# One-hots of the routing on VectorE, and another order of work where attention ends and the experts begin

## The chip, the cores and the metric

The kernel runs on one core of one Trainium2 chip. The metric is the device time of one launch in microseconds; the kernel before takes 539.12 us (median of 3 runs, 538.48 to 539.36). TensorE (PE in the profile) multiplies matrices, VectorE (DVE), ScalarE (ACT) and GpSimd (POOL) do elementwise work, SyncE (SP) issues most of the transfers. Each engine works off its own queue in order; between engines there are semaphores.

## The reference

A gated linear attention (mLSTM) over 2 batches, 8 heads, 768 steps and head size 40; then a mixture of 8 experts of which each of the 1536 tokens takes its best 2; then one wide layer for all tokens.

```python
for t in range(S):                                  # attention, per batch and head
    m_new = np.maximum(f_gate[t] + m, i_gate[t])
    C = exp(f_gate[t] + m - m_new) * C + exp(i_gate[t] - m_new) * outer(v[t], k[t])
    n = exp(f_gate[t] + m - m_new) * n + exp(i_gate[t] - m_new) * k[t]
    y[t] = sigmoid(o_gate[t]) * (C @ q[t]) / max(abs(n @ q[t]), 1.0)
logits = x @ w_gate + log1p(exp(x @ w_noise)) * noise   # x: [1536, 320]
top2, weights = two largest per token, softmax over the two
out[tokens of e] += weight * (relu(x @ w1[e]) @ w2[e])  # w1 320x1024, w2 1024x320, per expert
h = out @ w_in                                          # 320x2048
y = (h * clip(h + 3, 0, 6) / 6) @ w_out                 # 2048x320
```

## The kernel before, in words

Everything is one program with an order written out by hand: the order of the calls is the order in each engine's queue.

**Attention.** The 768 steps are cut into NT = 12 chunks of 64 steps; with two batches a chunk has 128 tokens. For chunk n the main loop (L1077) calls `pmul(n + 1)` (VectorE: scores times decay, into P), `inter(n)` (TensorE: query times the state Sb), `state(n)` (TensorE: keys times values; VectorE: the new Sb), `norm2(n - 1)` (VectorE: the finished output x of the chunk before, written to DRAM as Xd), `scores(n + 2)`, `values(n)` and `xpose(n - 1)` (TensorE: P times values; three transposes of x, L412), `expo(n + 2)` (TensorE: the exponents, its last matmuls at L271; ScalarE: dd), `logits(n - 1)` (TensorE: gate logits, L426), `kscale` (ScalarE: scaled keys kt), `norm_eg(n)` and `norm_pv(n)` (VectorE: sums and denominators; GpSimd: od). Between them `w_load`, `w_hi` and `w_lo` fetch weights of experts 0 and 1 into the four RAW buffers and split them into two parts (ScalarE and VectorE).

**Routing.** `route(m)` works on the logits of chunks 2m and 2m + 1. It is a generator: `step()` lets every running one go on to its next `yield`, and so puts a small instruction or two between the other work. It first copies the logits (zg), needs ScalarE for a softplus (u; the first VectorE operation on it is L451), finds the two largest, counts with small matmuls (L488 to L495) how many tokens each expert has so far, and gets a slot for each token and choice. Then it writes the token numbers into a table: two one-hot matrices LO (which of 128 rows) and HV (which of 32 columns, times the token number's two parts) are multiplied by four matmuls at L562, and the product is added to `slot`. `spot` counts places at which TensorE has work enough in front of the next small matmuls; a routing waits in its `yield` loop until `spot` has gone on by 2 (SPI) since its one-hots, or by SP = 4 since the last count. `until(m)` runs steps until m routings are in the table (`found`). The table of the first eight chunks (CUT) is turned into the index `idx[0]`, by which `gather` (GpSimd, an indirect transfer) fetches the x rows of the first 256 tokens of experts 0 and 1.

For routings 0 to 4 the one-hots are twelve GpSimd instructions (L541 to L544); for the last, routing 5, they are four VectorE instructions (L546 to L554).

**End of attention (L1120 to L1158).** The last two chunks are written out one call after the other: all values, norms, transposes and logits of chunks 10 and 11, `until` the table of eight chunks, `gather`, `xprep` (transposes of the gathered x, L828, and their split into XH and XL), and between them `dummy` matmuls, whose result nobody reads.

**Experts.** A unit is an expert with up to 416 tokens; expert 0 has a first unit of 256 tokens. A unit has eight steps f: `L1` (eight matmuls, L891, relu to hb by ScalarE, the remainder by VectorE, L897), and two steps later `L2` (six matmuls, L927 to L929). `bg(i, f, fn)` hangs a call behind step f of unit i, `bga` one right after its `L1`. `step` calls, weight splits (WS), gathers and the `xprep` of the next unit hang there. `open_late` gives the memory of attention to the second weight set SB.

Of the kernel before, what the change touches and what calls it, by code (L numbers as in the profile page):

```python
# [13 lines left out]
BF = mybir.dt.bfloat16  # L14
# [4 lines left out]
OP = mybir.AluOpType  # L19
# [4 lines left out]
B, H, S, D = 2, 8, 768, 40  # L24
# [19 lines left out]
LATE = 256  # L44
XP = (2, 3, 5, 6)
VSPLIT = {}
WS = ((-1, 0), (0, 3), (0, 4), (0, 5, 'h'), (1, 0, 'l'), (1, 1), (1, 1), (1, 3), (1, 5), (1, 7), (2, 1))
TROWS = CAP + 11 * 128
OVB = 22
OV = OVB * 128  # L50
# [16 lines left out]
def mlstm_moe_mlp(ctx, tc, qk, kv, on, gf, gf4, wg, nz, w1, w2, w_in, w_out, cf, cb, ci, out):  # L67
# [17 lines left out]
    def open_psd():  # L85
        nonlocal psd
        psa_cm.__exit__(None, None, None)
        psd = ctx.enter_context(tc.tile_pool(name="psd", bufs=1, space=PSUM))
# [151 lines left out]
    gens = []  # L240
    spot, counted = [0], [0, -2]

    def step(k=1):
        for _ in range(k):
            for g_ in list(gens):
                if next(g_, "end") == "end":
                    gens.remove(g_)
# [40 lines left out]
    def pmul(n):  # L288
        d = Pt[n][1]
        s4 = s4t.pop(n)  # L290
        P = att.tile([128, 8, 64], F32, name="P", bufs=3)
        V.tensor_tensor(P.rearrange("p (x a) t -> p x a t", x=2), s4, d.rearrange("p (x a) t -> p x a t", x=2), OP.mult)
        Pt[n] = P
# [41 lines left out]
    def values(n, hs):  # L335
        pv, _, vv = y_ps[n]
        for h in hs:
            for b in range(B):
                T.matmul(pv[rows[b], h, :], Pt[n][rows[b], h, :], vv[rows[b], h, :], start=True, stop=True)
# [5 lines left out]
    def dummy(k, b):  # L345
        p = bank(b)
        for _ in range(k):
            T.matmul(p, identb, cbt[:, 0:512], start=True, stop=True)
# [5 lines left out]
    def norm_eg(n):  # L354
        it = y_ps[n][1]
        y = att2.tile([128, 8, V1], F32, name="y", bufs=2)
        if n:
            V.tensor_tensor(y.rearrange("p (x a) c -> p x a c", x=2), it,
                            eG[:, n].rearrange("p (x a) -> p x a", x=2)[:, :, :, None].to_broadcast([128, 2, 4, V1]), OP.mult)
        ya[n] = y  # L360

    def norm_pv(n):
        y = ya[n]
        if n:
            V.tensor_tensor(y, y, y_ps[n][0], OP.add)
        else:
            V.tensor_copy(y, y_ps[n][0])
        o = att2.tile([128, 8, D], F32, name="od", bufs=2)
        G.tensor_tensor(o, ont[:, n].rearrange("p (h d) -> p h d", h=8), y[:, :, 0:D], OP.mult)
        step()  # L370
        den = att.tile([128, 8], F32, name="den", bufs=2)
        V.tensor_scalar(den, y[:, :, D], -1.0, 1.0, OP.mult, OP.max)
        step()
        V.tensor_tensor(den, den, y[:, :, D], OP.max)
        step()
        rd = att.tile([128, 8], F32, name="rd", bufs=2)
        V.reciprocal(rd, den)
        step()
        yt[n] = o, rd

    def norm2(n):
        o, rd = yt[n]
        x = att2.tile([128, XW], F32, name="x", bufs=4)
        V.tensor_tensor(x[:, 0:DM].rearrange("p (a x d) -> p x a d", a=4, x=2), o.rearrange("p (x a) d -> p x a d", x=2),
                        rd.rearrange("p (x a) -> p x a", x=2)[:, :, :, None].to_broadcast([128, 2, 4, D]), OP.mult)
        A.copy(x[:, DM:XW], x[:, 256:DM])
        xt[n] = x
        nc.sync.dma_start(Xd[n * 128:(n + 1) * 128], x)
# [9 lines left out]
    SLE = const.tile([128, NT, 2], I32, name="SLE")  # L398
    SLY = const.tile([128, NT, 2], I32, name="SLY")
    WAB = const.tile([128, NT, 2], F32, name="WAB")  # L400
    run = const.tile([128, E], BF, name="run")
    V.memset(run, 0.0)
    adj = const.tile([128, E], F32, name="adj")
# [4 lines left out]
    def xpose(n, b=6):  # L408
        p = bank(b)
        for k in range(3):  # L410
            w = 128 if k < 2 else 64
            T.transpose(p[0:w, k * 128:k * 128 + 128], xt[n][:, k * 128:k * 128 + w], ident)  # L412
        t = att2.tile([128, 3, 128], F32, name="xT", bufs=2)
        A.copy(t[:, 0:2], p[:, 0:256].rearrange("p (k t) -> p k t", k=2))
        A.copy(t[0:64, 2], p[0:64, 256:384])
        xT[n] = t
# [19 lines left out]
    def small(shape, name, dt=F32, bufs=2):  # L436
        return const.tile(shape, dt, name=name, bufs=bufs)

    def route(m):
# [95 lines left out]
        V.scalar_tensor_tensor(lh[:, 1], sli, 7, h1, OP.bitwise_and, OP.bitwise_or)  # L535
        LO = small([128, 4, 128], "LO", BF, 1)
        HV = small([128, 4, 2, 32], "HV", BF, 1)
        if m < NT // 2 - 1:
            lf = small([128, 2, 4], "lf")
            V.tensor_copy(lf, lh)  # L540
            for j in range(4):  # L541
                G.tensor_scalar(LO[:, j], iota128, lf[:, 0, j:j + 1], None, OP.is_equal)
                for x, v in enumerate((pcol, nval[:, 2 * m + j // 2:2 * m + j // 2 + 1])):
                    G.tensor_scalar(HV[:, j, x], iota128[:, 0:32], lf[:, 1, j:j + 1], v, OP.is_equal, OP.mult)  # L544
        else:
            V.tensor_tensor(LO, iota128[:, None, :].to_broadcast([128, 4, 128]),  # L546
                            lh[:, 0, :, None].to_broadcast([128, 4, 128]), OP.is_equal)
            yield
            H = small([128, 4, 32], "H", BF, 1)
            V.tensor_tensor(H, iota128[:, None, 0:32].to_broadcast([128, 4, 32]),  # L550
                            lh[:, 1, :, None].to_broadcast([128, 4, 32]), OP.is_equal)
            yield
            V.tensor_scalar(HV[:, :, 0], H, pcol, None, OP.mult)
            V.tensor_tensor(HV[:, :, 1].rearrange("p (n k) c -> p n k c", n=2), H.rearrange("p (n k) c -> p n k c", n=2),  # L554
                            nval[:, 2 * m:2 * m + 2, None, None].to_broadcast([128, 2, 2, 32]), OP.mult)
        at = spot[0]
        yield
        while spot[0] < at + SPI and not now[0]:
# [296 lines left out]
    def xprep(u, i, b=5):  # L855
        if u.e < 8:
            xsplit(u, i, XG[:, (u.xo + i) % 4], u.tiles[i][1], b)
        else:
            xsplit(u, i, x2t[4 * (u.e - 8) + i], 128, b)
# [215 lines left out]
    expo(1)  # L1075
    scores(1)
    for n in range(NT - 2):  # L1077
        pmul(n + 1)
        step(2)
        inter(n)  # L1080
        state(n)
        if n == 1:
            later_exponents()
            G.tensor_copy(adj, iota8)
        if n + 4 < NT:
            load_qk(n + 4)
        if 0 < n < NT - 3:
            load_kv(n + 3)
        if n % 2 == 0 and n + 2 < NT:
            load_on(n + 2)  # L1090
        if n >= 1:
            norm2(n - 1)
            step()
        w_lo(WL[n] if n < len(WL) else 0)
        scores(n + 2)
        values(n, range(8))
        if n >= 1:
            xpose(n - 1)
        expo(n + 2)
        for _ in range(WD[n] if n < len(WD) else 0):  # L1100
            w_load()
        w_hi(WH[n] if n < len(WH) else 0)
        if n == 1:
            decays(4, NT)
        if n + 3 >= NT:
            dummy(DUM[0], 4)
        if n >= 1:
            logits(n - 1)
        kscale(n + 2)
        if n == 0:  # L1110
            for i in range(3):
                gate(0, i)
        for i in ((0,), (1, 2))[n % 2]:
            gate(n // 2 * 2 + 2, i)
        norm_eg(n)
        step(2)
        norm_pv(n)
        if n >= 2 and n % 2 == 0:
            gens.append(route(n // 2 - 1))
# [6 lines left out]
    w_load()  # L1126
    step()
    values(n, range(8))
    norm_eg(n)
    step(2)  # L1130
    inter(n + 1, 4, s4p)
    norm_pv(n)
    spot[0] += 2
    norm_eg(n + 1)
    step(2)
    values(n + 1, range(8))
    open_psd()
    xpose(n - 1)
    norm2(n)
    norm_pv(n + 1)  # L1140
    spot[0] += 2
    xpose(n, 5)
    logits(n - 1)
    until(CUT[0] // 2)
    gather(units[0])
    norm2(n + 1)
    gens.append(route(NT // 2 - 2))
    dummy(DUM[1], 2)
    logits(n)
    dummy(DUM[2], 2)  # L1150
    xpose(n + 1, 6)
    step(3)
    xprep(units[0], 0, 3)
    logits(n + 1)
    gens.append(route(NT // 2 - 1))
    dummy(DUM[3], 5)
    xprep(units[0], 1, 2)
    dummy(DUM[4], 6)  # L1158

    LAG = 2  # L1160

    def bg(i, f, fn, *a):
        units[i].bg.setdefault(f, []).append((fn, a))
# [27 lines left out]
        sets[1] = Halves(late, "SB")  # L1191
        xbufs(late, 1)

    open_late()
    bg(0, 0, gather, units[1])
    for f in range(8):
        bg(0, f, step, 6)
    for i, f, *c in WS:
        for g_ in {'h': (w_hi,), 'l': (w_lo, w_load)}[c[0]] if c else (w_split,):
            if i < 0:  # L1200
                g_()
            else:
                bg(i, f, g_)
    bg(0, 7, until, NT // 2)
    bg(1, 1, gather, units[2])
    bg(1, 2, gather, units[3], 0, 1)
    bg(1, 7, gather, units[3], 2, 3)
    for i in range(3, M0 - 1):
        bg(i, 0, gather, units[i + 1])
# [139 lines left out]
```

## Time and profile before

| | us |
|---|---|
| median of 3 runs (lowest, highest) | 539.12 (538.48, 539.36) |
| the profiled execution | 538.7 |
| its span, first to last instruction | 536.9 |
| first matmul of expert 0 (L891) | 123.44 |
| TensorE busy | 494.1 |
| VectorE busy | 341.1 |
| ScalarE busy | 231.7 |
| GpSimd busy | 129.2 |

Busy time is the time in which an engine has at least one instruction in work; matmuls overlap, so a busy TensorE is not one at its peak. "Idle before" an instruction is the time that its engine had nothing to do ahead of it, with the instruction that released it. The granted clock is given as a share of 2.4 GHz: 0.50 is 1.2 GHz. Times in the rows below are us from the start of the span unless they are marked ns.

### The profile page before, as it was taken

What the parts mean: (1) busy time and instruction counts of PE and PEld (TensorE: products, weight loads), DVE (VectorE), ACT (ScalarE), POOL (GpSimd) and SP (SyncE); (2) the same over time, 40 slices, a digit from 0 to 9 for tenths busy, and PEclk for the clock granted to TensorE, in tenths of its full rate; (3) what the DMA queues carried; (4) which work ended last, traced back from release to release, by engine and by line L of the source; (5) the groups of instructions that cost most, each with busy time, mean ns of one, the idle gap of its engine ahead of it and who ended that gap; (6) DMA issues with size and microseconds to landing.
All of it is one profiled execution on the core that took longest, in us unless ns stands there. A gap on an engine that the chain in (4) does not pass through costs nothing. (4 is left out here: it accounts for less than half of the span.)

```text
span 536.9 us, 11617 instructions
## 1 busy us (share of the span) xinstructions
PE 494.1 (92%) x4547; PEld 449.1 (84%) x4547; DVE 341.1 (64%) x874; ACT 231.7 (43%) x483; POOL 129.2 (24%) x178
## 2 busy tenths in 40 slices
PE   5799867868699999999999999989999999999996
PEld 2687656646699999999999999979989899899985
DVE  7547766727476587878787877468697434353433
ACT  2346547215254454545454553255564334333322
POOL 2434455263330420202111002377400100000000
PEclk9555555559699999999999999999999999999999
DMA  9858663233277479888988769697722600010011
GB/s 187 206 170 234 167 191 117 71 95 93 79 219 219 151 271 292 290 284 290 273 302 275 267 183 319 205 295 227 241 99 80 214 0 1 1 31 20 13 37 49
DMA packets 41531, 90.76 MB, mean 169 GB/s; under 512 B 5233, under 2 KB 23985, under 8 KB 41473
## 3 DMA queue, kind: packets, MB, share of 16 engines
q1 hardware_dynamic: 34960, 69.07, 41.1%
q0 software_dynamic: 5696, 19.67, 11.9%
q10 hardware_dynamic: 816, 1.25, 1.1%
q8 instruction: 36, 0.59, 0.5%
q14 instruction: 23, 0.18, 0.1%
HBM read 67.16 MB, written 22.68 MB: 167 GB/s over the span
## 5 line engine op out<-in xcount | busy, mean ns | idle before, releaser
L906 DVE SCALAR_TENSOR_TENSOR r<-r,bank 128x512 f32<-128x512 f32 (+1 forms) x56 | 34.2, 611 | 80.1 <-ACT r L905 79.6
L894 ACT ACTIVATE hb<-bank 128x416 fp32r<-128x416 f32 (+2 forms) x80 | 35.6, 446 | 95.9 <-PE bank L891 82.7
L905 ACT ACTIVATE r<-bank,cft 128x512 f32<-128x512 f32 (+1 forms) x56 | 35.0, 626 | 95.5 <-PE bank L891 92.3
L891 PE MATMUL bank<-XH,SB 128*128 128x416 f32 (+3 forms) x280 | 75.6, 340 | 0.3 <-PEq L991 0.3
L891 PE MATMUL bank<-XL,SB 128*128 128x416 f32 (+3 forms) x192 | 66.9, 349 | 0.0
L818 POOL DMA_INDIRECT XG<-Xd,idx x32 | 33.1, 1034 | 127.5 <-PE bank L828 116.7
L927 PE MATMUL bank<-SB,hb 128*128 128x320 f32 x192 | 61.9, 322 | 1.0 <-ACT hb L878 1.0
L927 PE MATMUL bank<-SA,hb 128*128 128x320 f32 x192 | 61.3, 319 | 0.0
L929 PE MATMUL bank<-SA,hb 128*128 128x320 f32 x192 | 59.7, 311 | 0.1
L928 PE MATMUL bank<-SA,hb 128*128 128x320 f32 x192 | 59.6, 310 | 0.0
L929 PE MATMUL bank<-SB,hb 128*128 128x320 f32 x192 | 59.3, 309 | 0.0
L928 PE MATMUL bank<-SB,hb 128*128 128x320 f32 x192 | 59.2, 308 | 0.0
L891 PEld LDWEIGHTS bank<-XH,SB 128*128 128x128 f32 x280 | 50.3, 189 | 4.6 <-issue 0.6
L891 PE MATMUL bank<-XH,SA 128*128 128x416 f32 (+2 forms) x200 | 51.2, 329 | 0.1
L891 PE MATMUL bank<-XL,SA 128*128 128x416 f32 (+2 forms) x120 | 39.3, 329 | 0.1
L891 PEld LDWEIGHTS bank<-XH,SA 128*128 128x128 f32 x200 | 36.5, 196 | 1.9 <-ACT XH L829 0.6
L927 PEld LDWEIGHTS bank<-SB,hb 128*128 128x128 f32 x192 | 36.2, 188 | 2.1 <-ACT hb L878 1.2
L891 PEld LDWEIGHTS bank<-XL,SB 128*128 128x128 f32 x192 | 36.2, 188 | 2.0
L927 PEld LDWEIGHTS bank<-SA,hb 128*128 128x128 f32 x192 | 36.4, 190 | 1.1
L928 PEld LDWEIGHTS bank<-SA,hb 128*128 128x128 f32 x192 | 36.4, 190 | 0.9
L928 PEld LDWEIGHTS bank<-SB,hb 128*128 128x128 f32 x192 | 36.2, 189 | 0.6
L929 PEld LDWEIGHTS bank<-SA,hb 128*128 128x128 f32 x192 | 36.3, 189 | 0.3 <-DVE hb L879 0.3
(225 smaller groups left out, 1113.8 us busy)
## 6 DMA issues: line engine op xcount, KB each, us to landing
raw<-in_w_dram SPq DMA_DIRECT2D x18, 640.0 KB, 4.8
raw<-in_w_dram SPq DMA_DIRECT2D x18, 512.0 KB, 5.6
craw<-in_w_in_dram SPq DMA_DIRECT2D x8, 640.0 KB, 6.4
craw<-in_w_out_dram SPq DMA_DIRECT2D x8, 640.0 KB, 6.4
raw<-in_w_dram SPq DMA_DIRECT2D x18, 256.0 KB, 4.3
qk<-in_qk_dram SPq DMA_DIRECT2D x22, 192.0 KB, 4.3
Yd<-yo SPq DMA_DIRECT2D x24, 160.0 KB, 4.6
kv<-in_kv_dram SPq DMA_DIRECT2D x11, 324.0 KB, 5.0
```

The costliest lines, as they stand in the source:

```text
L818: G.indirect_dma_start(out=XG[0:n, (u.xo + i) % 4, :], out_offset=None, in_=Xd[0:CUT[u.i] * 128] if early else Xd[:, :], in_offset=bass.In ...
L891: T.matmul(p, a, b, start=(i == 0), stop=(i == 7))
L894: A.activation(hb[:, 0:N], p, AF.Relu)
L905: A.activation(r, p, AF.Relu, bias=three)
L906: V.scalar_tensor_tensor(r, r, 6.0, p, OP.min, OP.mult)
L927: T.matmul(p, h, wh, start=s, stop=False)
L928: T.matmul(p, h, wl, start=False, stop=False)
L929: T.matmul(p, hb[:, lo:lo + n], wh, start=False, stop=t)
```

## The change

1. The one-hots of all routings are made by VectorE. The slot halves go to bf16 (`lf`), a bf16 copy of the row numbers 0 to 127 (`iotab`, copied once by GpSimd in chunk 1) replaces the fp32 one, and there are four more `yield`s between the instructions.
2. In chunk 9 `step` counts double (`pace`) until chunk 11's values, `spot` goes on by two more, and the two dummies are gone.
3. The end of attention has another order: transposes of chunk 9 right after the values of chunk 10, then `until` and the `gather` for expert 0, its `xprep` ahead of the values of chunk 11, and expert 0 behind the transposes of chunk 10. All dummies are gone.
4. The logits of chunk 10, output, transposes and logits of chunk 11 and the last routing hang in expert 0's first three steps, and so does `open_late`. The weight splits, the `until` for all routings and the gathers for the later units hang one step or two later.

```diff
-WS = ((-1, 0), (0, 3), (0, 4), (0, 5, 'h'), (1, 0, 'l'), (1, 1), ...)
+WS = ((0, 2), (0, 3), (0, 4), (0, 6, 'h'), (1, 0, 'l'), (1, 1), ...)
+    pace = [1]
     def step(k=1):
-        for _ in range(k):
+        for _ in range(k * pace[0]):
...
-        if m < NT // 2 - 1:
-            lf = small([128, 2, 4], "lf")
-            V.tensor_copy(lf, lh)
-            for j in range(4):
-                G.tensor_scalar(LO[:, j], iota128, lf[:, 0, j:j + 1], None, OP.is_equal)
-                for x, v in enumerate((pcol, nval[:, 2 * m + j // 2:2 * m + j // 2 + 1])):
-                    G.tensor_scalar(HV[:, j, x], iota128[:, 0:32], lf[:, 1, j:j + 1], v, OP.is_equal, OP.mult)
-        else:
-            V.tensor_tensor(LO, iota128[:, None, :].to_broadcast([128, 4, 128]),
-                            lh[:, 0, :, None].to_broadcast([128, 4, 128]), OP.is_equal)
...
+        yield
+        lf = small([128, 2, 4], "lf", BF)
+        V.tensor_copy(lf, lh)
+        yield
+        V.tensor_tensor(LO, iotab[:, None, :].to_broadcast([128, 4, 128]),
+                        lf[:, 0, :, None].to_broadcast([128, 4, 128]), OP.is_equal)
+        yield
+        H = small([128, 4, 32], "H", BF, 1)
+        V.tensor_tensor(H, iotab[:, None, 0:32].to_broadcast([128, 4, 32]),
+                        lf[:, 1, :, None].to_broadcast([128, 4, 32]), OP.is_equal)
+        yield
+        V.tensor_scalar(HV[:, :, 0], H, pcol, None, OP.mult)
+        V.tensor_tensor(HV[:, :, 1]..., H..., nval[:, 2 * m:2 * m + 2, ...], OP.mult)
...
     for n in range(NT - 2):
+        if n == NT - 3:
+            pace[0] = 2
...
+            G.tensor_copy(iotab, iota128)
...
-        if n + 3 >= NT:
-            dummy(DUM[0], 4)
...
+        if n == NT - 3:
+            spot[0] += 2
         step(2)
...
     values(n, range(8))
+    xpose(n - 1)
     norm_eg(n)
-    step(2)
     inter(n + 1, 4, s4p)
-    norm_pv(n)
-    spot[0] += 2
-    norm_eg(n + 1)
-    step(2)
-    values(n + 1, range(8))
-    open_psd()
-    xpose(n - 1)
-    norm2(n)
-    norm_pv(n + 1)
-    spot[0] += 2
-    xpose(n, 5)
-    logits(n - 1)
     until(CUT[0] // 2)
     gather(units[0])
-    norm2(n + 1)
+    norm_pv(n)
+    logits(n - 1)
     gens.append(route(NT // 2 - 2))
-    dummy(DUM[1], 2)
-    logits(n)
-    dummy(DUM[2], 2)
-    xpose(n + 1, 6)
-    step(3)
-    xprep(units[0], 0, 3)
-    logits(n + 1)
-    gens.append(route(NT // 2 - 1))
-    dummy(DUM[3], 5)
-    xprep(units[0], 1, 2)
-    dummy(DUM[4], 6)
+    norm_eg(n + 1)
+    spot[0] += 2
+    step(2)
+    norm2(n)
+    xprep(units[0], 0, 6)
+    xprep(units[0], 1, 5)
+    values(n + 1, range(8))
+    pace[0] = 1
+    open_psd()
+    xpose(n)
+    norm_pv(n + 1)
...
-    open_late()
+    bga(0, 0, logits, n)
+    bga(0, 0, norm2, n + 1)
+    bga(0, 1, xpose, n + 1, 5)
+    bga(0, 2, logits, n + 1)
+    bga(0, 2, last_route)
     bg(0, 0, gather, units[1])
+    bg(0, 2, open_late)
     for f in range(8):
         bg(0, f, step, 6)
+    bg(1, 0, step, 8)
...
-    bg(0, 7, until, NT // 2)
-    bg(1, 1, gather, units[2])
-    bg(1, 2, gather, units[3], 0, 1)
+    bg(1, 1, until, NT // 2)
+    bg(1, 2, gather, units[2])
+    bg(1, 3, gather, units[3], 0, 1)
```

## Rows read from the trace of the kernel before

**Rows 1.** The page: busy time of the engines, and the granted TensorE clock in 40 slices.

```profile
PE 494.1 (92%) x4547; PEld 449.1 (84%) x4547; DVE 341.1 (64%) x874; ACT 231.7 (43%) x483; POOL 129.2 (24%) x178
...
PEclk9555555559699999999999999999999999999999
```

**Rows 2.** Waits of TensorE, whole span: total us, times, longest.

```profile
PE bank L562 <- POOL HV L544: 24.8, 19, 2.7
```

**Rows 3.** Windows of two stretches: busy time and instructions of each engine, clock, DMA.

```profile
57.00:69.00 12.00, 12.00 (x268) 9.82 (x270) 11.31 (x43) 6.50 (x20) 3.64 (x4) 0.50 0.63 181
69.00:76.00 7.00, 2.82 (x84) 2.28 (x88) 1.72 (x11) 4.12 (x14) 5.95 (x12) 0.50 0.73 197
```

**Rows 4.** Timeline of TensorE, chunks 3 to 7: start, duration, instructions, [idle before, releaser].

```profile
36.27 0.61 PE L271 MATMUL bank<-RWG,SEL 128*128 128x64 bf16 x8
...
41.56 0.87 PE L412 MATMUL bank<-cft,x 128*128 128x128 f32 x3
...
59.60 0.90 PE L412 MATMUL bank<-cft,x 128*128 128x128 f32 x3
...
68.03 0.61 PE L271 MATMUL bank<-RWG,SEL 128*128 128x64 bf16 x8
...
72.64 0.21 PE L562 MATMUL bank<-HV,LO 128*128 128x64 bf16 x1 [1.27 <-POOL HV L544]
...
78.48 0.90 PE L412 MATMUL bank<-cft,x 128*128 128x128 f32 x3
```

**Rows 5.** Timeline of VectorE, chunks 3 and 7.

```profile
39.92 0.18 DVE L451 TENSOR_SCALAR w<-u 128x16 f32<-128x16 f32 x1 [1.53 <-ACT u L446]
...
40.92 0.48 DVE L384 TENSOR_TENSOR x<-od,rd 128x320 f32<-128x320 f32 x1
...
72.97 0.22 DVE L451 TENSOR_SCALAR w<-u 128x16 f32<-128x16 f32 x1 [2.79 <-ACT u L446]
```

**Rows 6.** Groups of GpSimd by line: busy us, mean ns, idle before.

```profile
L544 POOL TENSOR_SCALAR HV<-cft,lf 128x32 bf16<-128x32 f32 x40 | 18.4, 469 | 0.0
L542 POOL TENSOR_SCALAR LO<-cft,lf 128x128 bf16<-128x128 f32 x20 | 12.8, 640 | 8.9 <-DVE lf L540 7.3 <-DVE rd L377 1.1 <-DVE den L374 0.4
```

**Rows 7.** Timeline of VectorE: the one-hots of the last routing.

```profile
141.94 0.69 DVE L546 TENSOR_TENSOR LO<-cft,lh 128x512 bf16<-128x512 f32 x1
...
142.87 0.29 DVE L550 TENSOR_TENSOR H<-cft,lh 128x128 bf16<-128x128 f32 x1
...
143.60 0.24 DVE L553 TENSOR_SCALAR HV<-H,cft 128x128 bf16<-128x128 bf16 x1
143.76 0.28 DVE L554 TENSOR_TENSOR HV<-H,cft 128x128 bf16<-128x128 bf16 x1
```

**Rows 8.** Groups of TensorE by line, end of the attention part.

```profile
L348 PE MATMUL bank<-cbt 128*128 128x512 bf16 x10 | 4.5, 548 | 0.7 <-ACT dd L274 0.7
```

**Rows 9.** Timeline of TensorE, end of the attention part.

```profile
118.68 0.66 PE L426 MATMUL bank<-wgt,xT 128*32 128x16 f32 x24
...
120.10 0.85 PE L412 MATMUL bank<-cft,x 128*128 128x128 f32 x3
...
123.44 0.38 PE L891 MATMUL bank<-XH,SA 128*128 128x256 f32 x1
```

**Rows 10.** Timeline of GpSimd, and the landing times of tile XG's transfers.

```profile
117.02 1.09 POOL L818 DMA_INDIRECT XG<-Xd,idx  x1 [0.22 <-DVE WAB L573]
...
DMA to landing us min/median/max: 2.4/3.1/3.8
```

**Rows 11.** Windows of expert 0, columns as in rows 3.

```profile
123.44:132.00 8.56, 8.32 (x63) 7.69 (x63) 7.38 (x50) 4.87 (x13) 1.24 (x2) 1.00 0.43 123
132.00:139.33 7.33, 0.77 (x9) 0.56 (x9) 1.60 (x3) 0.63 (x1) 6.81 (x12) 0.70 0.27 73
139.33:145.10 5.77, 5.77 (x30) 5.77 (x29) 4.53 (x21) 2.02 (x3) 0.00 (x0) 0.50 0.25 94
145.10:180.00 34.90, 34.90 (x273) 34.17 (x272) 22.48 (x67) 15.79 (x33) 10.12 (x11) 1.00 0.69 214
```

More of the change, by code (lines that the diff above doesn't have):

```diff
@@ L46 @@
 VSPLIT = {}
-WS = ((-1, 0), (0, 3), (0, 4), (0, 5, 'h'), (1, 0, 'l'), (1, 1), (1, 1), (1, 3), (1, 5), (1, 7), (2, 1))
+WS = ((0, 2), (0, 3), (0, 4), (0, 6, 'h'), (1, 0, 'l'), (1, 1), (1, 1), (1, 3), (1, 5), (1, 7), (2, 1))
 TROWS = CAP + 11 * 128
@@ L400, in mlstm_moe_mlp @@
     WAB = const.tile([128, NT, 2], F32, name="WAB")
+    iotab = const.tile([128, 128], BF, name="iotab")
     run = const.tile([128, E], BF, name="run")
@@ L537, in route @@
         HV = small([128, 4, 2, 32], "HV", BF, 1)
-        if m < NT // 2 - 1:
-            lf = small([128, 2, 4], "lf")
-            V.tensor_copy(lf, lh)
-            for j in range(4):
-                G.tensor_scalar(LO[:, j], iota128, lf[:, 0, j:j + 1], None, OP.is_equal)
-                for x, v in enumerate((pcol, nval[:, 2 * m + j // 2:2 * m + j // 2 + 1])):
-                    G.tensor_scalar(HV[:, j, x], iota128[:, 0:32], lf[:, 1, j:j + 1], v, OP.is_equal, OP.mult)
-        else:
-            V.tensor_tensor(LO, iota128[:, None, :].to_broadcast([128, 4, 128]),
-                            lh[:, 0, :, None].to_broadcast([128, 4, 128]), OP.is_equal)
[L548 to L555, printed above, removed]
+        yield
[10 more added lines that the diff above has]
+        V.tensor_scalar(HV[:, :, 0], H, pcol, None, OP.mult)
+        V.tensor_tensor(HV[:, :, 1].rearrange("p (n k) c -> p n k c", n=2), H.rearrange("p (n k) c -> p n k c", n=2),
+                        nval[:, 2 * m:2 * m + 2, None, None].to_broadcast([128, 2, 2, 32]), OP.mult)
         at = spot[0]
@@ L1192, in open_late, with last_route @@
         xbufs(late, 1)
-    open_late()
+    def last_route():
+        gens.append(route(NT // 2 - 1))
+    bga(0, 0, logits, n)
[3 more added lines that the diff above has]
+    bga(0, 2, last_route)
     bg(0, 0, gather, units[1])
+    bg(0, 2, open_late)
     for f in range(8):
         bg(0, f, step, 6)
+    bg(1, 0, step, 8)
     for i, f, *c in WS:
         for g_ in {'h': (w_hi,), 'l': (w_lo, w_load)}[c[0]] if c else (w_split,):
[L1200 to L1203, printed above, removed]
-    bg(0, 7, until, NT // 2)
-    bg(1, 1, gather, units[2])
-    bg(1, 2, gather, units[3], 0, 1)
+            bg(i, f, g_)
+    bg(1, 1, until, NT // 2)
+    bg(1, 2, gather, units[2])
+    bg(1, 3, gather, units[3], 0, 1)
     bg(1, 7, gather, units[3], 2, 3)
```

## The prediction

> **What bounds the kernel now.** I read the page first: TensorE is busy 92% of the span, and its clock row is at 5 from the second slice to the ninth (13 to 121 us) and at 9 after that, apart from one slice [rows 1]. So there are two parts: attention until about 123 us at the low level (1.2 GHz), the experts after it at the high one (2.4 GHz). Next the waits of TensorE: one line carries nearly all, 24.8 us in 19 waits for GpSimd's one-hots (L562 for HV) [rows 2]. The windows then show how they lie: for 12 us TensorE is busy 12.00, and in the next 7 us only 2.82, while GpSimd is busy 5.95 [rows 3]. GpSimd's groups say why: one routing has 4 LO at 0.64 us and 8 HV at 0.47 us, 6.3 us in a row, and there are five such routings (20 LO, 40 HV) [rows 6]. TensorE's queue is in order, so everything behind L562 waits. Four of these stalls lie in attention, the fifth in expert 0 (132.00 to 139.33, TensorE busy 0.77 of 7.33 us); behind it the clock is at 0.50 for 5.77 us more, then back at 1.00 [rows 11]. From there on TensorE is busy all the time, so what comes off before it comes off the end.
>
> **The change, part by part.** The sum goes against the profiled execution, 538.7 us: a span of 536.9, and 1.8 around it. The median of the three runs is 539.1, 0.4 above.
>
> *The stalls.* 24.8 us of waits go [rows 2]. In expert 0 they are the idle 7.33 - 0.77 = 6.56 us [rows 11], so 18.2 are left in attention.
>
> *The one-hots on VectorE.* The last routing does them there already: 0.69 + 0.29 + 0.24 + 0.28 = 1.5 us [rows 7]. The new ones read bf16, which no row shows for LO; bounds for the four together are 0.7 us (four operations at the 0.18 us of a small one [rows 5]) and GpSimd's 6.3. I take 1.5, from the nearest row. The Trainium skill (VectorE: DVE Perf Modes, The perf-mode tier table) gives a bf16 two-tensor operation twice the fp32 rate; its Side-by-side section asks step 1 of that mode, and lf is broadcast. The 0.28 us of L554, bf16 in and out with a broadcast operand, is no faster than H's 0.29, which agrees with that [rows 7]. At double rate some 0.25 us would go from each LO, by an estimate from that page, and the sum would be about half a microsecond lower.
>
> *What VectorE then makes late in the loop.* Per two chunks (59.60 to 78.48, 18.9 us now [rows 4]) it is busy 11.31 + 1.72 = 13.0 us, 14.5 with the one-hots, where TensorE has 12.00 + 2.82 = 14.8 us of work [rows 3]: nearly equal. It is in order too, and its first routing step after zg waits for ScalarE's u (2.79 us idle before L451); behind that stand Sb, x and the weight split [rows 5]. Today the L562 stall hides this. In chunk 3, which has no stall, L451 starts 3.0 us behind the end of the exponent matmuls (36.27 + 0.61), x follows 1.0 us later and ends at 41.40, just before its transposes at 41.56, 4.7 us behind the exponents [rows 4, 5]. In chunk 7 ScalarE has weights and kt to do first: L451 comes 4.3 us behind the exponents (72.97 against 68.64) [rows 4, 5]; with HV (0.45) in between, x ends at 4.3 + 1.0 + 0.45 + 0.5 = 6.3 us, where TensorE needs it at 4.7. New wait: 1.6 us, in chunks 5 and 7 each. By my count of the step() calls, the four added yields push L562 of routings 0 and 1 one chunk further, so that these two no longer wait.
> In chunk 9 step() counts double. Some 13 more small operations come before x; four small ones and a large one took 1.0 us [rows 5], so 0.13 us each, 1.7 us: wait 3.1. In chunk 10 L562 of routing 3 stands right behind inter and state; about 4 us of VectorE work (ten small operations at 0.13, two norms at 0.5, the 1.5 of the one-hots) meet inter and state, by an estimate 1.7 of the 4.7 us above: wait 2.3, and 0.4 on x behind that.
>
> *The earlier gather.* Found is set by then, so until() issues nothing. From the last L562: 0.6 us to idx (three small operations), 1.09 for the first GpSimd issue, 3.1 to landing [rows 10], 4.8 us; the second 1.3 later. Behind L562 TensorE has values, transposes, inter and logits, which I put at 4.2 of the 7.4 us of a chunk (half of 14.8), then the transposes of the first half: wait 1.0 (0 to 2.5 with landings of 2.4 to 3.8), and the last values and expert 0 stand behind it. New waits altogether 1.6 + 1.6 + 3.1 + 2.3 + 0.4 + 1.0 = 10.0 us; bounds 1 (the gather's alone) and 18 (as long as the old ones).
>
> *Small terms.* The L562 matmuls no longer come singly: 4 x 0.21 [rows 4] become something between 0.21 (all overlapped) and 0.84, I take 0.3: 2.2 us for four routings, 0.5 in expert 0. The ten dummies go, 4.5 + 0.7 us of idle [rows 8], of which I count 5.0. Logits twice and one transposition, 1.7 us net of overlap, leave the end of attention [rows 9]. The copy to iotab on GpSimd (a LO is as large, 0.64 us [rows 6]) lies beside matmuls in chunk 1: nothing, at most 0.6. The moved write of x, gather and weight loads keep their order in SP's and GpSimd's queues; weights 5 to 8 are in RAW before expert 0 either way; the late split could wait for the last x write: 0 to 1.
>
> *Expert 0.* It starts cold: the dummies are gone. The low clock costs 5.77 / 2 = 2.9 us behind the stall today [rows 11], and I take the same at the start: no difference. Bounds: 1.5 and 6. Logits and a transposition between its matmuls: 2.1 us cold, 1.05 of warm work. VectorE has in its first 8.56 us 7.38 us of work without a TensorE stall worth naming (0.24 us) [rows 11]; two rounds of one-hots, 3 us, come on top while three weight splits run: 1.5 us (0 to 5).
>
> *Sum.* Start of expert 0: 123.4 - 18.2 - 2.2 - 5.0 - 1.7 + 10.0 = 106.3. Rest: 536.9 - 123.4 = 413.5 (start [rows 9]); - 6.6 - 0.5 + 1.05 + 1.5 = 408.9. Span 515.2, time 517.0: 21.7 us less, which on the median makes 517.4.
>
> **Rivals.**
> *No new waits.* The row that speaks for it: TensorE did 12 us without a gap with VectorE busy 11.31 of them [rows 3]. Against: those 12 us followed a stall, and the wait for u repeats. It saves 9 of the 10.0 and the 1.5: 507.
> *VectorE becomes the bound* in chunks 9 and 10 and in expert 0. For: 14.5 against 14.8 us per two chunks, doubled steps, 7.38 of 8.56 us [rows 3, 11]. Against: its idle time before u is used by the steps in between. Waits in chunks 9 and 10 double (+5.8), expert 0 stalls 3.5 more: 527.
> *The wait only changes hands*: at L562 TensorE waits for VectorE as long as for GpSimd, because the one-hots stand behind splits, norms and u. Then the 24.8 stay and the other new waits don't come: 538.7 - 5.0 - 1.7 + 2.1 = 534. Against: 1.5 us instead of 6.3.
> *Slower: the clock stays low in the experts.* Small gaps that VectorE leaves between expert matmuls keep the granted clock at 0.50; every 2 us so spent cost 1, so the gain of 21.7 is gone after 43 us more at 0.50, about the first three units. If it lasts 60: 517.4 + 30 = 547. For: attention stays at 0.50 though TensorE is busy 12.00 of 12 [rows 3]. Against: with VectorE busy 7.38 of 8.56 the clock was 1.00, and after the stall it rose within 5.77 us of expert matmuls [rows 11]. The Trainium skill (TensorE: Matmul & The Clock Gate, A second HAM failure mode: psum-queue depth-cycling) describes micro-idles between groups of matmuls that make the clock go back and forth; by that rule this rival would be the case, and no row here shows it for expert matmuls.
>
> **Chances.** Forecast 0.53 (its own range 511 to 523), no new waits 0.20, VectorE bound 0.17, changed hands 0.05, clock 0.04, no change 0.01. The range for 8 in 10 leaves out the last ones and the far ends of the second and third: 508 to 527. A run tells 0.2% from no change; faster by more than that: 0.53 + 0.20 + 0.17 + 0.05 = 0.95; same 0.01; slower 0.04.
>
> **What would show it.** Right: no wait of L562 for GpSimd; L562 of routings 0 and 1 a chunk later without a wait; TensorE's waits on x at L412 in chunks 5, 7 and 9, and one on HV in chunk 10; first expert matmul near 106 us; the clock at 1.00 some 6 us behind it; experts 2 to 7 as long as before. Wrong: expert 0 starting before 100 (no new waits) or behind 112 (VectorE bound), or later units longer than now, which would mean that what was saved is lost to weights or clock.

## The result, and the profile after

The changed kernel takes 524.21 us (median of 4 runs, 523.2 to 525.3) where the kernel before, beside it on the same chip, takes 539.19 (538.48 to 539.36): a ratio of 0.9725 [0.9701, 0.9749]. It is 15.0 us faster; the forecast was 21.7 us less, 517.4. The time lies inside the range, 6.8 us above the forecast.

The page of the changed kernel: busy time of the engines (answers to [rows 1]).

```profile
PE 490.8 (94%) x4537; PEld 448.7 (86%) x4537; DVE 346.8 (66%) x895; ACT 231.9 (44%) x483; POOL 99.2 (19%) x119
...
PEclk9555555558999999999999999999999999999999
```

GpSimd has lost 30.0 us (129.2 before), VectorE has gained 5.7. TensorE's waits over the whole span, changed kernel (total us, times, longest; answers to [rows 2]):

```profile
PE bank L561 <- DVE HV L553: 6.5, 4, 2.5
PE bank L415 <- DVE x L386: 5.1, 3, 2.2
...
PE bank L827 <- DMA XG<-Xd,idx: 3.8, 2, 3.3
PE bank L415 <- DVE dl L484: 1.8, 1, 1.8
...
PE s4p L265 <- DVE P L294: 0.8, 2, 0.4
```

The 24.8 us on GpSimd's HV [rows 2] are gone as a line. What stands in their place is VectorE (HV, x, dl, P) and the gather. One of the three waits on x, of 2.2 us, lies in chunk 1 and was there before. Where the new ones lie, TensorE's timeline of the changed kernel says (start, duration, instructions, [idle before, releaser]):

```profile
58.06 0.87 PE L415 MATMUL bank<-cft,x 128*128 128x128 f32 x3 [1.36 <-DVE x L386]
...
62.12 0.40 PE L561 MATMUL bank<-HV,LO 128*128 128x64 bf16 x4
...
62.97 0.81 PE L265 MATMUL s4p<-qk 40*64 40x64 f32 x20 [0.37 <-DVE P L294]
...
73.91 0.87 PE L415 MATMUL bank<-cft,x 128*128 128x128 f32 x3 [1.48 <-DVE x L386]
...
86.75 0.37 PE L561 MATMUL bank<-HV,LO 128*128 128x64 bf16 x4 [0.97 <-DVE HV L553]
91.63 0.87 PE L415 MATMUL bank<-cft,x 128*128 128x128 f32 x3 [1.78 <-DVE dl L484]
98.30 0.37 PE L561 MATMUL bank<-HV,LO 128*128 128x64 bf16 x4 [2.34 <-DVE HV L553]
103.54 0.87 PE L827 MATMUL bank<-cft,XG 128*128 128x128 f32 x3 [0.56 <-DMA XG<-Xd,idx]
107.67 0.88 PE L827 MATMUL bank<-cft,XG 128*128 128x128 f32 x3 [3.26 <-DMA XG<-Xd,idx]
110.89 0.56 PE L890 MATMUL bank<-XH,SA 128*128 128x256 f32 x1
...
124.67 0.28 PE L561 MATMUL bank<-HV,LO 128*128 128x64 bf16 x4 [2.52 <-DVE HV L553]
...
131.65 0.28 PE L561 MATMUL bank<-HV,LO 128*128 128x64 bf16 x4 [0.64 <-DVE HV L553]
```

The reader is to see three things. The waits lie where the prediction put them: x in chunks 5 and 7, the doubled steps of chunk 9, HV in chunk 10, and none at L561 of the first two routings. The largest of all is one that it had put at 1.0 us, the gather (0.56 + 3.26). And expert 0 has a wait of 2.52 us in its middle.

Windows of the changed kernel (columns as in [rows 3]; the first is all of attention, the rest expert 0 and what follows, against [rows 11]):

```profile
0.00:110.89 110.89, 88.83 (x1974) 71.08 (x1975) 78.24 (x276) 49.26 (x141) 29.79 (x41) 0.56 0.64 174
110.89:115.20 4.31, 4.31 (x42) 4.01 (x41) 2.84 (x18) 1.27 (x5) 2.77 (x3) 0.50 0.24 61
115.30:125.40 10.10, 7.58 (x88) 7.12 (x87) 6.29 (x38) 4.38 (x12) 0.52 (x1) 1.00 0.29 95
125.50:128.90 3.40, 3.40 (x16) 3.40 (x16) 3.40 (x15) 1.86 (x4) 0.00 (x0) 0.50 0.39 84
129.00:160.00 31.00, 30.05 (x234) 28.97 (x234) 23.36 (x67) 15.36 (x29) 5.81 (x6) 1.00 0.69 207
```

The granted clock rises 4.3 us behind the first expert matmul and falls once more, 0.8 us behind the end of the wait of 2.52 us, for 3.4 us. The same first window of the kernel before, up to its start of expert 0:

```profile
0.00:123.44 123.44, 94.23 (x2036) 72.89 (x2036) 74.20 (x261) 50.44 (x147) 55.67 (x91) 0.57 0.59 158
```

Expert 0 starts 12.55 us sooner: TensorE is idle 110.89 - 88.83 = 22.1 us in place of 29.2 (7.1 less) and busy 5.4 us less. From there to the end the two kernels need nearly the same, 523.5 - 110.89 = 412.6 us against 413.5.

### The profile page after: what moved, and what is told of

Same layout as the page of the kernel before. It is cut to its first block, busy times and chain, and to the rows that moved or that the text cites. A ratio compares the mean times of both kernels' runs of the same rounds, so it can differ in the third digit from the quotient of the medians.

```text
span 523.5 us, 11555 instructions
## 1 busy us (share of the span) xinstructions
PE 490.8 (94%) x4537; PEld 448.7 (86%) x4537; DVE 346.8 (66%) x895; ACT 231.9 (44%) x483; POOL 99.2 (19%) x119
## 3 DMA queue, kind: packets, MB, share of 16 engines
q10 hardware_dynamic: 816, 1.25, 1.1%
```

## The experiments

Each ratio is to the kernel before on the same chip, with its 95% interval; that kernel's median was 539.0 to 541.3 by the chip, so ratios are compared and not times.

**1 and 2. The two halves alone: who earns the 15 us?** `onehots_only` is the kernel before, with its order and its dummies, and the VectorE one-hots (bf16 `iotab`, the four `yield`s). `order_only` is the changed kernel with the GpSimd one-hots of the kernel before.

```diff
# onehots_only, on the kernel before (order_only: this hunk undone in the changed kernel)
-        if m < NT // 2 - 1:
-            lf = small([128, 2, 4], "lf")
...
+        yield
+        lf = small([128, 2, 4], "lf", BF)
+        V.tensor_copy(lf, lh)
+        yield
+        V.tensor_tensor(LO, iotab[:, None, :].to_broadcast([128, 4, 128]),
+                        lf[:, 0, :, None].to_broadcast([128, 4, 128]), OP.is_equal)
...
+            G.tensor_copy(iotab, iota128)
```

> The kernel before with one part of the change alone: all one-hots on VectorE (with the bf16 row numbers and the four yields), the old order and the dummies kept. Theory (nearly all of the gain is the one-hots, and the new order at the end gives back some of it: a cold clock, a gather with transfers in its way, a routing wait in expert 0): the four attention stalls of 18.2 us shrink to about 4, the stall of 6.6 us in expert 0 to at most 2 and its cold stretch goes; expert 0 starts warm near 108; time 516 to 520, below the changed kernel's 524.2. Rival (the new order carries a good part of the gain): 527 to 532.

> The changed kernel with the one-hots of routings 0 to 4 put back to GpSimd: the order, the double steps and the missing dummies alone. Theory: the stalls of L562 for GpSimd come back at 4 to 6.5 us each, the one of routing 3 now right ahead of the gather; time 533 to 541, ratio to before 0.99 to 1.00. Rival (the order hides the GpSimd chain behind other work): 526 or less.

Measured: `onehots_only` 519.74 us, 0.9641 [0.9611, 0.967]; `order_only` 539.77 us, 1.0017 [0.9999, 1.0035]. The one-hots, with their four `yield`s, carry the whole gain, and more than it: without the new order the kernel is faster than with it, and the intervals of 0.9641 and 0.9725 don't touch. The new order alone gives nothing. TensorE's waits in `order_only`, first row:

```profile
PE bank L565 <- POOL HV L547: 25.7, 19, 2.6
```

Its stalls are as long as before (24.8), so expert 0 starts at 123.23 us, as in the kernel before. In `onehots_only` the same view has HV with only 3.5 us:

```profile
PE bank L413 <- DVE x L384: 5.7, 4, 2.2
...
PE bank L559 <- DVE HV L551: 3.5, 3, 1.3
```

The new waits on x in chunks 5 and 7 are there as well (1.55 and 1.49 us), so they belong to the one-hots. Expert 0 starts later than in the changed kernel (112.09 against 110.89), but the rest takes 520.7 - 112.09 = 408.6 us against 412.6. The order saves 1.2 us ahead of the experts and loses 4.0 in them.

One rival inside this half is untested. With the four `yield`s the table matmuls of routings 0 and 1 stand at 62.42 and 78.27 us, behind the transposes of their chunk; in the kernel before they begin at 52.64 and 71.16. No run has the `yield`s with GpSimd's one-hots, so how much of the gain is the later place and how much the faster engine is not shown.

**3. The gather: does a weight load stand beside it?** In the changed kernel the load of 640 KB of weights is issued at 101.04 us, 0.2 us behind the second gather (SyncE's and GpSimd's timelines):

```profile
100.86 0.98 POOL L817 DMA_INDIRECT XG<-Xd,idx  x1 [0.31 <-issue]
...
101.04 0.43 SPq L636 DMA_DIRECT2D raw<-in_w_dram  x1
```

`load_behind` issues it behind the last values.

```diff
     norm2(n - 1)
-    w_load()
     step()
...
     values(n + 1, range(8))
+    w_load()
```

> The changed kernel with one weight load (640 KB) issued behind the last values instead of in chunk 10. Theory (the 3.26 us wait of the transposes for the second half of the gather is the transfer queueing behind that load): the wait falls below 1 us, time 2 to 3 us below the changed kernel, about 521.5. Rival (the gather is late by its own chain, GpSimd's issue and a landing time of 4 to 7 us): the wait stays within 0.5 us, time 524.

Measured: 520.47 us, 0.9659 [0.9633, 0.9686], some 3.5 us better than 0.9725. The landing of XG's transfers between 90 and 140 us, in the changed kernel:

```profile
DMA to landing us min/median/max: 2.4/3.1/6.7
```

and in `load_behind`:

```profile
DMA to landing us min/median/max: 2.6/3.1/4.7
```

TensorE's timeline there has the second half at 1.42 us of wait in place of 3.26:

```profile
102.87 0.87 PE L827 MATMUL bank<-cft,XG 128*128 128x128 f32 x3 [0.41 <-DMA XG<-Xd,idx]
105.17 0.87 PE L827 MATMUL bank<-cft,XG 128*128 128x128 f32 x3 [1.42 <-DMA XG<-Xd,idx]
```

The load beside it made the gather slower by 2 us. It is not all of it: 4.7 us is still above the 2.4 to 3.8 of the kernel before [rows 10], and the wait was expected below 1 us. In `onehots_only`, where no weight load stands near, the slowest landing between 90 and 140 us is 4.5 us, and TensorE waits 1.74 us for the gather. Both halves together wait 2.0 us less in `load_behind` than in the changed kernel (0.56 + 3.26 to 0.41 + 1.42); what the rest of the 3.5 us is, no run says.

**4 and 6. The wait in expert 0: can its place be changed?** The wait of 2.52 us is on routing 4's one-hots. `later_table` lets the table matmuls of that routing stand further behind them; `count_sooner` starts its counts one place sooner.

```diff
# later_table
-        while spot[0] < at + SPI and not now[0]:
+        while spot[0] < at + (4 if m == 4 else SPI) and not now[0]:
# count_sooner
-        while counted[0] < m or not now[0] and (spot[0] < at + 2 or spot[0] < counted[1] + SP):
+        while counted[0] < m or not now[0] and (spot[0] < at + (1 if m == 4 else 2) or spot[0] < counted[1] + SP):
```

> The changed kernel with the table matmuls of routing 4 (in expert 0) two places later, that is one step f. Theory (this wait of 2.5 us and the low clock behind it are a matter of the place alone): the wait goes, the clock stays at 1.00, time 3 to 4 us lower, about 520.5. Rival (VectorE and ScalarE are behind with everything there: relu number 4 starts 4 us after its matmuls, behind the split and e2): the wait moves to the second matmuls that need hb, time within 1 us of 524.

> The changed kernel with the count of routing 4 in expert 0 one place earlier (behind one L1 less). Theory (VectorE idles 3 us between 114.5 and 118.4 because the routing waits for its place, and then has one-hots, both routings and splits at once): the one-hots of routing 4 come ahead of the first split, the wait of 2.52 us falls below 1 and the clock does not fall again; time 2 to 4 us lower, about 521. Rival (the work is only moved, and a later small matmul or hb is late instead): within 1 us of 524.2.

Measured: 0.9707 [0.9682, 0.9732] and 0.9721 [0.9687, 0.9755], neither to be told from 0.9725. The wait moves. TensorE's timeline of expert 0 in `later_table`:

```profile
123.43 0.17 PE L491 MATMUL bank<-mk,cbt 128*128 128x16 bf16 x1 [1.82 <-DVE mk L480]
131.09 0.28 PE L561 MATMUL bank<-HV,LO 128*128 128x64 bf16 x4 [1.22 <-DVE HV L553]
```

and in `count_sooner`:

```profile
120.10 0.28 PE L561 MATMUL bank<-HV,LO 128*128 128x64 bf16 x4 [0.21 <-DVE HV L553]
123.28 0.17 PE L491 MATMUL bank<-mk,cbt 128*128 128x16 bf16 x1 [0.99 <-DVE mk L480]
130.67 0.28 PE L561 MATMUL bank<-HV,LO 128*128 128x64 bf16 x4 [2.72 <-DVE HV L553]
```

The sums are 3.0 and 3.9 us against 2.52 + 0.64 = 3.2. VectorE has all of the last two routings, the splits of the weights and the remainders of hb in its queue here: it is late with whatever TensorE asks for first. So the theory that the place of the table decides fell. That VectorE is full here, the rival, fits both runs: the waits move and the time stays.

**5. u earlier: are the waits on x those for ScalarE?** The prediction put the waits of chunks 5 and 7 down to VectorE waiting for u behind ScalarE's `kscale` and `gate`. In even chunks, where a routing begins, the first routing step goes ahead of them.

```diff
-        kscale(n + 2)
...
+        def scale():
+            kscale(n + 2)
...
+        early = n < 2 or n % 2
+        if early:
+            scale()
         norm_eg(n)
...
             gens.append(route(n // 2 - 1))
+            next(gens[-1])
+        if not early:
+            scale()
```

> The changed kernel, where in even chunks the first step of a new routing (zg, and ScalarE's u) goes ahead of ScalarE's kt scaling and gate instead of behind them. Theory (VectorE stands 1.5 to 2.1 us idle for u in chunks 5, 7 and 9, and this makes x late for its transposes by 1.36, 1.48 and 1.78 us): the idle time before L454 goes, the waits on x fall below 0.5 each, time 3 to 4.5 us lower, about 520.5. Rival (VectorE is simply full there): the waits on x stay or move to P, time within 1 us of 524.2.

Measured: 520.93 us on a chip where the kernel before takes 541.28, 0.9618 [0.9588, 0.9649]: 5.8 us better than 0.9725. VectorE's timeline at L454, the same routing first in the changed kernel, then in `u_sooner`:

```profile
56.20 0.17 DVE L454 TENSOR_SCALAR w<-u 128x16 f32<-128x16 f32 x1 [2.08 <-ACT u L449]
```

```profile
52.92 0.17 DVE L454 TENSOR_SCALAR w<-u 128x16 f32<-128x16 f32 x1
```

In the loop VectorE no longer waits for u, and TensorE's waits on x in chunks 5 and 7 and on P are gone; of all of them 0.32 us is left, in chunk 9:

```profile
87.99 0.87 PE L415 MATMUL bank<-cft,x 128*128 128x128 f32 x3 [0.32 <-DVE dl L484]
```

That is 5.1 us of waits less. In expert 0 a wait on HV grows (0.64 to 2.19 us), and the clock does not fall a second time there. The step of the prediction is shown.

**7. The dummies in the gap of the gather.** In the changed kernel six dummy matmuls go between the two `xprep`, where TensorE waits for 3.26 us.

```diff
     xprep(units[0], 0, 6)
+    dummy(6, 5)
     xprep(units[0], 1, 5)
```

> The changed kernel with six dummy matmuls (128x512, bf16) between the two transposition groups of the gathered x, where TensorE waits 3.26 us for the transfer. Theory of the clock (expert 0 starts cold for want of dummies): they lie in the wait, the clock rises up to 4 us sooner, time 1 to 2 us lower, about 522.5. Rival (these few do not bring the clock up, or push the transposes back): 524 to 525.

Measured: 525.05 us, 0.9699 [0.967, 0.9727]: not to be told from 0.9725. The wait falls to 0.87 us, but that is only the dummies lying in it, and the clock is still at 0.50 for 3.8 us behind the first expert matmul (110.34 to 114.10), 4.3 in the changed kernel. The theory that they make the clock rise sooner fell.

**8 and 9. The mends put together, in either order.** `onehots_u_sooner` is experiment 1 with the edit of 5; `order_both_mended` is the changed kernel with the edits of 3 and 5.

```diff
# order_both_mended, on the changed kernel
+            next(gens[-1])
+        if not early:
+            scale()
...
-    w_load()
...
     values(n + 1, range(8))
+    w_load()
```

> The one-hots alone (old order, dummies kept) together with the sooner u. Theory: its waits on x in chunks 5, 7 and 9 go as in the changed kernel, about 4 us: 515.5 to 516.5, the fastest so far. Rival (VectorE is full): 519 to 520.

> The changed kernel with both mendings: the weight load behind the last values, and the sooner u. Theory (the two waits are independent and add): ratio to before 0.955 to 0.957, level with the one-hots in the old order and the sooner u (0.9557), so that the new order is worth nothing even when mended, because VectorE is full in expert 0. Rival (mended, the order shows its gain of dummies and waiting time): 0.950 or less.

Measured: 0.9557 [0.9525, 0.9589] and 0.9576 [0.9551, 0.9601], level. The waits add up: 3.5 and 5.8 us from 0.9725 make 0.955 (9.3 / 540 = 0.017). With u sooner in both and the load moved in the new order, the new order is as good as the old one; no run shows it better. Its second fall of the clock is still there:

```profile
118.72:122.13 3.41, 3.41 (x17) 3.41 (x16) 3.41 (x15) 1.94 (x4) 0.00 (x0) 0.50 0.30 77
```

**10. The dummies, in the old order.** `onehots_u_sooner` without any dummy.

```diff
-        if n + 3 >= NT:
-            dummy(DUM[0], 4)
...
-    dummy(DUM[1], 2)
...
-    dummy(DUM[2], 2)
...
-    dummy(DUM[3], 5)
...
-    dummy(DUM[4], 6)
```

> The one-hots in the old order with the sooner u, without the ten dummy matmuls. Theory of the clock (the dummies buy warm expert matmuls): the clock rises 2 to 4 us later behind the first expert matmul, and as they lie mostly in waits, time 1 to 2 us above the same kernel with them (ratio 0.958 to 0.960). Rival (they cost TensorE time, as my sum counted 5.0 us for them): 3 us or more below it, ratio 0.951 or less.

Measured: 513.93 us, 0.9532 [0.9507, 0.9558], the lowest of all kernels run. The clock does rise later, as the clock's theory said, but the loss of time that it forecast (0.958 to 0.960) fell. The rival's 0.951 is not reached, though the interval takes it in. Beside 0.9557 the intervals overlap, so no run shows that the dummies bring anything, nor that they cost something. The windows say how the two sides balance; first with dummies (`onehots_u_sooner`: attention, and the cold start of expert 0):

```profile
0.00:105.74 105.74, 88.53 (x2033) 69.88 (x2036) 78.89 (x277) 50.16 (x147) 32.16 (x44) 0.62 0.67 184
...
105.74:107.20 1.46, 1.46 (x6) 1.29 (x6) 1.11 (x3) 0.90 (x1) 0.95 (x2) 0.50 0.45 115
```

and without (`no_dummies`):

```profile
0.00:103.77 103.77, 86.20 (x2026) 69.19 (x2026) 79.10 (x277) 50.37 (x147) 31.76 (x44) 0.60 0.67 188
...
103.77:109.88 6.11, 6.11 (x27) 5.94 (x28) 5.17 (x34) 2.51 (x8) 1.31 (x2) 0.50 0.60 172
```

Without dummies attention is 2.0 us shorter (0.4 of it stands ahead of the first dummy already: the transposes of chunk 9 start at 84.80 us and 85.16) and TensorE 2.3 us less busy. The clock stays low 6.11 us instead of 1.46 in expert 0, which by the halved rate costs (6.11 - 1.46) / 2 = 2.3 us. That would be a draw, as the two ratios are. The profiled executions are further apart: from the start of expert 0 on, the kernel without dummies needs 510.8 - 103.77 = 407.0 us, the other 516.0 - 105.74 = 410.3. They come from two chips, and no run says what these 3.3 us are.

## Why the prediction was right, and by which steps it was 6.8 us off

In the profiled executions the miss is 523.5 - 515.2 = 8.3 us: 110.89 - 106.3 = 4.6 at the start of expert 0, 412.6 - 408.9 = 3.7 behind it. (The profiled execution, 525.3 us, is the slowest of the four; so about 1 us of the 8.3 is chance.)

Of the 4.6, new waits make 2.5 (12.5 us for 10.0) and work that was not saved 3.5 (5.4 us for 8.9); other waits of attention are 1.4 us shorter than before. 0.7 of the 4.6 stands ahead of all this: the transposes of chunk 3 start at 42.23 us, in the kernel before at 41.56, and in `load_behind`, the same program up to chunk 10, at 41.41. That part is chance.

**The stalls** went, as said. With GpSimd's one-hots put back they return in full (experiment 2), and VectorE's one-hots with their `yield`s bring the whole gain (experiment 1).

**The one-hots on VectorE**: 1.5 us forecast. VectorE's groups in `onehots_only`, six routings (busy us, mean ns, idle before):

```profile
L543 DVE TENSOR_TENSOR LO<-iotab,lf 128x512 bf16<-128x512 bf16 x6 | 4.1, 684 | 0.0
L551 DVE TENSOR_TENSOR HV<-H,cft 128x128 bf16<-128x128 bf16 x6 | 1.7, 283 | 0.0
L547 DVE TENSOR_TENSOR H<-iotab,lf 128x128 bf16<-128x128 bf16 x6 | 1.6, 274 | 0.0
L550 DVE TENSOR_SCALAR HV<-H,cft 128x128 bf16<-128x128 bf16 x6 | 1.5, 250 | 0.1
```

0.684 + 0.274 + 0.250 + 0.283 = 1.49 us for a routing. LO from bf16 takes 684 ns, from fp32 it took 0.69 us [rows 7]: bf16 bought nothing. The trace so agrees with what the Trainium skill (VectorE: DVE Perf Modes, Side-by-side) asks of the fast mode, step 1, which a broadcast operand doesn't have; the tier table alone would have had each LO some 0.25 us shorter, by the prediction's estimate. The row that the prediction gave for this, L554, does not show it: its second operand lies in `cft`, which is fp32. LO, with both operands in bf16, does.

**The new waits in the loop**: chunk 5 1.36 and chunk 7 1.48 (1.6 each forecast), chunk 9 1.78 on x (3.1), chunk 10 2.34 (2.3, and 0.4 on x that didn't come). Not forecast were 0.97 on the one-hots of routing 2 in chunk 9 and two on P, 0.37 and 0.40; the latter hang on the same u, for they go with it (experiment 5). Together 8.7 us for a forecast of 9.0. That VectorE's queue is held by ScalarE's u was the step that mattered, and it is shown.

**The gather** failed: 3.8 us for 1.0, beyond its bound of 2.5. The step reads "the second 1.3 later", with landings of 2.4 to 3.8 [rows 10]. Those landings were read where no load of that size was issued right behind the gather. The order of the queues had been looked at (unchanged), but not what shares their time once the gather has moved. The slowest landing took 6.7 us beside the load and 4.7 without it (experiment 3).

**The small terms** failed: 2.2 + 5.0 + 1.7 = 8.9 us less work for TensorE ahead of expert 0, measured 5.4. The dummies are the term that was too large: taken away alone, in the old order, they are worth 2.3 us of TensorE's busy time and 2.0 us of attention, not 5.0 (experiment 10). In the kernel before, the last 2.1 us ahead of expert 0 (121.30 to 123.44) ran at a granted clock of 1.00; in the changed kernel, without dummies, they run at 0.50. That their listed 4.5 us also overlap with neighbours and lie in waits is likely, but no run separates it.

**Expert 0** was mis-sized within its bounds. Forecast was 1.5 us for VectorE (0 to 5); measured are waits of 2.52 + 0.64 = 3.2, and 3.4 us at the low clock behind the longer one, which cost 1.7. The cold start was shorter, 4.3 us at 0.50 for 5.77 (0.7 less). The moved logits and transposition take 0.58 + 0.25 + 0.43 = 1.3 us up to the next expert matmul, for 1.05. That leaves about 0.8 of the 3.7 us unassigned; the moved splits and the spread of single executions are candidates, and no run separates them. The later units are as long as before, as forecast: from the start of one and the same transposition of a gathered x (156.17 us, 170.07 before) to the end it is 367.3 us, and 366.8 before.

**The rivals.** "No new waits" fell by the waits of chunks 5 to 10. "VectorE becomes the bound" was right in one place: in expert 0 waits only move (experiments 4 and 6). In chunks 9 and 10 they come to 0.97 + 1.78 + 2.34 = 5.1 us, where the forecast had 5.8 and this rival double. "The wait only changes hands" fell: HV has 6.5 us, not 24.8. The clock rival, too, had its mechanism and not its size: the clock did fall again among expert matmuls, for 3.4 us and not 60. The page that it leaned on (the Trainium skill, TensorE: Matmul & The Clock Gate, A second HAM failure mode) has the clock go back and forth at frequent micro-idles between groups of matmuls; the trace does not show that here, only one fall behind one pause of 2.52 us, and the clock at 1.00 from 129 to 160 us.

Behind the start of expert 0 the new order needs 4.0 us more than the old one (412.6 to 408.6). The rows account for that. At a granted clock of 0.50 the changed kernel spends 4.3 + 3.4 us of expert 0, `onehots_only` 2.7:

```profile
112.09:114.80 2.71, 2.71 (x12) 2.54 (x12) 2.01 (x5) 1.26 (x3) 0.98 (x2) 0.50 0.48 126
```

Half of the difference is 2.5 us; the moved logits and transposition take 1.3, and the waits on HV are 0.6 longer (3.2 to 1.25 + 1.32). No run takes one of the three away alone. What stays open is why the clock falls the second time, for which see the last section.

## What to carry to other kernels

When a long wait goes, read what the engines behind it had been hiding in it: here VectorE's in-order queue, held by a ScalarE result, came out at once, and having that result made a little sooner was worth 5.8 us, while the reordering is not shown to be worth anything. A transfer that is moved needs its landing time read beside the transfers that it will then meet, not where it stood alone. Price filler work by taking it out of a kernel, not by its listed busy time: the ten dummies were listed with 4.5 us and counted with 5.0, and taking them out was a draw.

## What the hardware showed that was not expected

The clock fell behind a TensorE pause inside warm expert work in six of the kernels with the new order: pauses of 2.52 us (the changed kernel), 2.47 (`load_behind`), 2.50 (`dummies_in_gap`), 2.46 (`order_both_mended`), 2.72 (`count_sooner`) and 1.82 (`later_table`). It fell some 0.5 to 0.9 us behind the end of the pause, while TensorE was busy, and was at 0.50 for 3.3 to 3.4 us. But in `u_sooner`, of the same order, it stayed at 1.00 through pauses of 2.50 and 2.19 us:

```profile
119.74 0.28 PE L561 MATMUL bank<-HV,LO 128*128 128x64 bf16 x4 [2.50 <-DVE HV L553]
126.72 0.28 PE L561 MATMUL bank<-HV,LO 128*128 128x64 bf16 x4 [2.19 <-DVE HV L553]
...
116.00:130.00 14.00, 9.31 (x79) 8.96 (x79) 11.85 (x54) 5.39 (x11) 1.55 (x2) 1.00 0.42 127
```

So the length of the pause alone does not decide, and what does is not shown. In `onehots_only`, with pauses of 1.25 and 1.32 us and VectorE just as full (7.49 of 7.60 us), it stayed too:

```profile
121.00:128.60 7.60, 5.12 (x45) 4.78 (x44) 7.49 (x30) 3.74 (x6) 0.00 (x0) 1.00 0.36 98
```

Single executions also have gaps before a matmul for which the profile names only "issue", that is, nothing that it shows was waited for: 2.03 us at 55.05 in `u_sooner`, and 2.6 to 3.3 us near 20.5 us in four of the kernels, where the changed kernel has 0.55. What makes them is not shown.
